# Linear attention, top-1 mixture of experts and a squared-ReLU FFN in one kernel: the decayed state enters by an identity matmul, and gate, row-transpose and weight-conversion steps change places

## The chip, the cores and the metric

The kernel runs on one core of a Trainium2 chip. A core has a matmul engine (PE, whose weight loads the profile lists apart as PEld), a vector engine (DVE), a scalar engine (ACT), GpSimd (POOL) and SyncE (SP), which issues most of the transfers. The metric is the device time of one execution in microseconds (us); lower is better.

## The reference

Three stages follow one another. B = 4 batches, H = 8 heads, S = 768 positions, head width 48, so 3072 tokens of width 384.

```python
for t in range(S):                                    # linear attention with decay
    state = alpha[:, :, t, :, None] * state + einsum('bhd,bhe->bhde', k[:, :, t], v[:, :, t])
    y[:, :, t] = einsum('bhd,bhde->bhe', q[:, :, t], state)
x = y as [3072, 384]
logits = x @ w_gate + modality_bias[modality_id]      # 8 experts, top 1
gate_w = softmax(logits) at the argmax
x = gate_w * (relu(x @ w1[e]) @ w2[e])                # 384 -> 1024 -> 384, e per token
h = x @ w_in                                          # 384 -> 2048
return (relu(h) ** 2) @ w_out                         # 2048 -> 384
```

All arrays are float32, but `w_in` and `w_out` are float64 and are made float32 on the chip.

## The kernel before, in words

The order of the instructions on every engine is the order in which the code is written; there is no scheduler. An engine runs its instructions in that order, and each waits for what it reads and for the buffer that it writes.

**Attention.** There are 24 tiles of 128 tokens, six to a batch, counted n = 0 to 23; the loop `for n in range(N)` runs over them. `prep(n)` does a tile's decay on DVE: two scans along the tokens (`acum`, line 448, and `rs`, line 452) and two products (`qt`, 454; `kt`, 456). `qk_mm` makes the scores (`sp`, line 469), which ACT copies (472) and POOL masks (474). `k_T` turns `kt` round (483). `kv_mm` makes a tile's own state in PSUM (`kv`, line 497); DVE adds the state carried from the tiles before (`st`, line 503) and multiplies by the tile's decay (`sd`, line 504; 506 for the first tile of a batch). ACT copies `sd` into a block-diagonal tile (`sbd`, 513 and 514), and `y_mm` makes the output from it and from the masked scores (523, 528). `kv`, `y` and the transposes' PSUM tile `x` have one buffer each. In iteration n the code writes `kv_mm(n)`, `qk_mm(n + 1)`, `k_T(n + 1)`, a first `ts()`, `prep(n + 3)`, a second `ts()`, `y_mm(n)`, `s_bd(n + 1)`, a third `ts()`. Lists of deferred steps hang on places of an iteration ("pre", "pool", "mid", "end"); `at(n, place, f)` adds one and `do(n, place)` runs them.

**Gate.** Tiles are taken in groups of 8, 8, 5 and 3. When a group's outputs are there, `gate_lg` makes its logits transposed (`lt`, line 206), ACT copies them, and PE transposes them back (`lg`, line 212). `gate_a` picks the expert (DVE, 219 to 228), `gate_b` counts ranks on PE (`rk`, 235), `gate_c` finishes the ranks, `gate_s` makes the gate weight `gw` (an exponential on ACT, line 261, then 263 to 266 on DVE). `ts()` takes the next tile from `todo_ts`, transposes it into rows on PE (`xtr`, 274), scales it by `gw` on ACT (`xb`, 278) and stores it to the DRAM array `xs`. `gate_bt` writes a tile's 128x128 selection matrix (286).

**Experts.** Slots 0 and 1 take 256 tokens each of the expert with the most tokens of the first two groups; slots 2 to 6 take 512 tokens and slot 7 256. For each slot POOL gathers rows of `xs` (604), PE transposes them (`xt`, 612 and 622), and ACT and DVE split them into a rounded part and a rest (`xh`, `xl`; lines 539, 540). Weights are split likewise (`w1h`, `w1l`, `w2h`, `w2l`) as they arrive: `push` queues loads, `pop` splits the oldest and issues the next, at most four in flight. Each product is three matmuls (`mm3`, lines 629 to 631). From slot 2 on, step f of a slot makes one eighth of the hidden width (`s1`: `hps`, then `hh` on ACT, 900, and `hl` on DVE, 901) and the second product of step f - 2 (`s2`).

**Conversion.** Between these steps `conv_tick((2, 0, 1))` stores one finished 128x512 piece of the float64 weights (`conv_store`, line 709), loads another (685), and converts a third: five DVE instructions (691 to 695), one on ACT (696), two on POOL (702, 703). There are 24 pieces. The result sits in a `cvt` tile; that tag has two buffers.

**Last FFN.** Six chunks of 512 tokens, 16 steps each. `m1` makes a step's hidden part (`h`), then `r` on ACT (977; it is allocated from the same two `cvt` buffers), its square on DVE (978), the rounded part on ACT (539) and the rest on DVE (540). `m2` (`acc`) follows `LAG` = 2 steps behind; of the last `TAIL` = 6 steps it is done tile by tile at the end, each output row scattered by POOL (1001).

Of the kernel before, what the change touches and what calls it, by code (L numbers as in the profile page):

```python
# [56 lines left out]
def body(ctx, tc, qka, v, alpha, mod, wg, mbias, w1, w2, w_in, w_out, out):  # L57
# [142 lines left out]
    def gate_lg(g, i0, i1):  # L200
        t0 = GROUPS[g][0]
        lt = ps_g.tile([128, 128], F32, tag="lt", name="lt")
        for p in range(NP):
            for i in range(i0, i1):
                q = slice(32 * (i - i0), 32 * (i - i0 + 1))
                PE.matmul(lt[q, :], wg_sb[:, p, :], yts[t0 + i][:, p, :], start=(p == 0), stop=(p == NP - 1))
        n = 32 * (i1 - i0)
        ls = gt.tile([128, 128], F32, tag="ls", name="ls")
        A.copy(ls[:n], lt[:n])
        if i0 == 0:  # L210
            gst[g] = dict(lg=ps_g.tile([128, GM, 32], F32, tag="rk", name="lg"))
        PE.transpose(gst[g]["lg"][:, i0:i1, :].rearrange("p t e -> p (t e)"), ls[:n], ident[:n, :n])

    def gate_a(g):
        t0, T = GROUPS[g]
# [24 lines left out]
    def gate_c(g):  # L240
# [14 lines left out]
        V.tensor_copy(lof, lo)  # L255
        gst[g]["lof"] = lof

    def gate_s(g):
        t0, T = GROUPS[g]
        ex = gt.tile([128, T, NE], F32, tag="ex", name="ex")  # L260
        A.activation(ex, gst[g]["dl"], AF.Exp)
# [226 lines left out]
    def kv_mm(n):  # L488
        c = n % NCH
        if c == NCH - 1:  # L490
            return
        vv, kT = vs[n], kTs.pop(n)
        kv = ps_a.tile([RP, NP, D], F32, tag="kv", name="kv")
        for p in range(NP):
            for j in range(2):
                w = 64 if j == 0 else D
                PE.matmul(kv[64 * j:64 * j + w, p, :], kT[:, p, 64 * j:64 * j + w], vv[:, 2 * p + j, :], start=True, stop=True)
        shp = [RP, NP, D]
        sd = at2.tile(shp, F32, tag="sd", name="sd")
        aen = preps[n]["ae"].to_broadcast(shp)  # L500
        if c > 0:
            st = at2.tile(shp, F32, tag="st", name="st")
            V.tensor_add(st, kv, sds[n])
            V.tensor_tensor(sd, st, aen, op=ALU.mult)
        else:
            V.tensor_tensor(sd, kv, aen, op=ALU.mult)
        sds[n + 1] = sd

    def s_bd(n):
# [237 lines left out]
    for n in range(N):  # L747
        if n + 4 < N:
            loaded[n + 4] = load(n + 4)
        if n + 3 < N:  # L750
            vs[n + 3] = load_v(n + 3)
        do(n, "pre")
        kv_mm(n)
        if n + 1 < N:
            qk_mm(n + 1)
            k_T(n + 1)
        do(n, "pool")
        ts()
        if n + 3 < N:
            preps[n + 3] = prep(n + 3)  # L760
        do(n, "mid")
        ts()
        if n > GROUPS[EG + 1][0] + 3:
            pop(2)
        if n == N - 1:
            x_T(0, 0)
            x_T(0, 1)
        y_mm(n)
        if n + 1 < N:
            s_bd(n + 1)  # L770
        ts()
        if n > 0:
            g, i = tile_group[n - 1]
            t0, T = GROUPS[g]
            if i % 4 == 3 or i == T - 1:
                gate_lg(g, i // 4 * 4, i + 1)
            if i == T - 1:
                gate_a(g)
                at(n + 1, "mid", lambda g=g: (gate_b(g), gate_s(g)))
                at(n + 1, "end", lambda g=g: gate_c(g))  # L780
                if g == EG:
                    at(n + 2, "mid", early_plan)
                    at(n + 3, "pre", lambda: push(wload(0)))
                    at(n + 4, "mid", lambda: early.append(first_ids(EARLY, 2, ids_e)))
                    at(n + 5, "pool", lambda: (early.pop()(), gather(0)))
                d = 4 if g == EG else 3
                for k in range(T):
                    at(n + 1 + k // 3, "end", lambda t=t0 + k: gate_bt(t))
                    at(n + 2 + k // d, "pre", lambda t=t0 + k: todo_ts.append(t))
        do(n, "end")  # L790
    for n in range(N, N + 4):
        for k in ("pre", "pool", "mid", "end"):
            do(n, k)
        while todo_ts:
            ts(True)
# [122 lines left out]
    for i in range(2, NSLOT):  # L918
        last = i == NSLOT - 1
        for f in range(8):  # L920
            if f == 0:
                if i > 2:
                    s2(i - 1, 6)
                drain(("w1", i - 1))
                soff[i] = offset(i)
                perm(i, soff[i])
                if last:
                    push(load_w1(WS, lambda k: wi32[k * 128:(k + 1) * 128, 0:1024]))
                else:
                    gather(i + 1)  # L930
                    push(wload(i))
            s1(i, f)
            if f > 0:
                pop()
            if f in ((0, 2, 4) if last else (0, 2, 3, 5)):
                conv_tick((2, 0, 1))
            if last and f == 2:
                push(load_w2(WS, lambda k: wo32[k * 256:(k + 1) * 256, :].rearrange("(f p) d -> p f d", p=128)))
            if f == 5:
                if last:  # L940
                    xx2[0] = xsplit(chunks[0], range(1))
                else:
                    x_T1(i + 1, 0)
            if f == 7:
                if last:
                    xx2[0] = xsplit(chunks[0], range(1, KD), xx2[0])
                else:
                    x_T1(i + 1, 1)
            if f == 1 and i > 2:
                s2(i - 1, 7)  # L950
            if f >= 2:
                s2(i, f - 2)
            if f == 7 and not last:
                x_T1(i + 1, 2)
# [12 lines left out]
    def m1(s):  # L967
# [281 lines left out]
```

## Time and profile before

| what | value |
|---|---|
| median of 3 runs | 813.72 us (812.34 to 813.73) |
| the profiled execution | 814.7 us, of which the span from first to last instruction is 813.0 us |
| PE busy | 764.5 us, 94% of the span |
| PE weight loads | 675.0 us, 83% |
| DVE busy | 499.6 us, 61% |
| ACT busy | 338.1 us, 42% |
| POOL busy | 182.2 us, 22% |
| mean granted clock of PE | 0.98 of full speed (full is 2.4 GHz, the other level 1.2 GHz) |

The shares are means over stages with different limits, so they say little of any one of them. Matmuls overlap in the records: the cost of one in a row of many is the distance between two starts, not its own duration.

### The profile page before, as it was taken

What the parts mean: (1) busy time and instruction counts of PE and PEld (TensorE: products, weight loads), DVE (VectorE), ACT (ScalarE), POOL (GpSimd) and SP (SyncE); (2) the same over time, 40 slices, a digit from 0 to 9 for tenths busy, and PEclk for the clock granted to TensorE, in tenths of its full rate; (3) what the DMA queues carried; (4) which work ended last, traced back from release to release, by engine and by line L of the source; (5) the groups of instructions that cost most, each with busy time, mean ns of one, the idle gap of its engine ahead of it and who ended that gap; (6) DMA issues with size and microseconds to landing.
All of it is one profiled execution on the core that took longest, in us unless ns stands there. A gap on an engine that the chain in (4) does not pass through costs nothing.

```text
span 813.0 us, 12791 instructions
## 1 busy us (share of the span) xinstructions
PE 764.5 (94%) x4975; PEld 675.0 (83%) x4975; DVE 499.6 (61%) x827; ACT 338.1 (42%) x622; POOL 182.2 (22%) x177
## 2 busy tenths in 40 slices
PE   7797877899899999999999999999999999999994
PEld 6686766789778888888899999999999999999984
DVE  7999799566787796877864444544454343343340
ACT  2454647634444444445653332332333233233230
POOL 6341423202655444533100010010001002002001
PEclk9897989999999999999999999999999999999998
DMA  8563856327898578678740030012000001000001
GB/s 231 157 179 110 254 156 228 120 92 216 170 246 265 159 257 196 180 231 121 214 130 1 1 116 26 1 53 91 1 10 31 1 1 40 0 1 30 10 0 44
DMA packets 42557, 88.78 MB, mean 109 GB/s; under 512 B 11149, under 2 KB 26535, under 8 KB 42487
## 3 DMA queue, kind: packets, MB, share of 16 engines
q1 hardware_dynamic: 39287, 78.04, 34.8%
q0 software_dynamic: 3200, 9.83, 3.7%
q8 instruction: 41, 0.67, 0.4%
q14 instruction: 29, 0.24, 0.1%
HBM read 72.10 MB, written 15.76 MB: 108 GB/s over the span
## 4 chain that ended last, share of the span: by engine, by line
PE 65%; DVE 2%; DMA 2%; issue 0%; ACT 0%; POOL 0%; POOLq 0%; DVEq 0%; SPq 0%
PE h L630 8%; PE h L631 8%; PE acc L631 8%; PE acc L629 8%; PE acc L630 8%; PE h L629 8%; PE hps L630 3%; PE oo L630 3%; PE hps L631 3%; PE hps L629 3%; PE oo L631 3%; PE oo L629 3%; DMA wo<-cvt 1%; DVE w1l L540 1%; PE xt L622 1%; DMA wi<-cvt 1%
## 5 line engine op out<-in xcount | busy, mean ns | idle before, releaser
L978 DVE TENSOR_TENSOR r<-r 128x512 f32<-128x512 f32 x96 | 66.5, 693 | 148.8 <-ACT r L977 148.6
L631 PE MATMUL acc<-w2h,hl 128*128 128x384 f32 x376 | 126.9, 338 | 0.0
L629 PE MATMUL acc<-w2h,hh 128*128 128x384 f32 x376 | 126.7, 337 | 0.0
L630 PE MATMUL acc<-w2l,hh 128*128 128x384 f32 x376 | 126.4, 336 | 0.0
L977 ACT ACTIVATE r<-h 128x512 f32<-128x512 f32 x96 | 57.4, 598 | 162.0 <-PE h L631 161.0
L631 PE MATMUL h<-xh,w1l 128*128 128x512 f32 x288 | 113.9, 396 | 0.0
L630 PE MATMUL h<-xl,w1h 128*128 128x512 f32 x288 | 113.7, 395 | 0.0
L629 PE MATMUL h<-xh,w1h 128*128 128x512 f32 x288 | 112.1, 389 | 0.0
L1001 POOL DMA_INDIRECT out_dram<-ob,pidx x24 | 24.6, 1026 | 385.9 <-ACT ob L999 348.1
L540 DVE TENSOR_TENSOR hl<-r,hh 128x512 fp32r<-128x512 f32 x94 | 65.1, 693 | 64.5 <-PE acc L631 39.8
L539 ACT CAST hh<-r 128x512 fp32r<-128x512 f32 x94 | 58.3, 620 | 75.6 <-DVE r L978 75.6
L629 PEld LDWEIGHTS acc<-w2h,hh 128*128 128x128 f32 x376 | 70.7, 188 | 4.0
L630 PEld LDWEIGHTS acc<-w2l,hh 128*128 128x128 f32 x376 | 70.6, 188 | 3.9
L631 PEld LDWEIGHTS acc<-w2h,hl 128*128 128x128 f32 x376 | 70.5, 188 | 0.0
L630 PE MATMUL hps<-xl,w1h 128*128 128x512 f32 (+1 forms) x192 | 68.1, 355 | 2.6 <-DVE xl L540 2.6
L630 PE MATMUL oo<-hl,w2h 128*128 128x512 f32 (+1 forms) x192 | 67.7, 353 | 1.9 <-DVE hl L901 1.7
L474 POOL TENSOR_SCALAR_AFFINE_SELECT pm<-pa 128x512 f32<-128x512 f32 x48 | 48.7, 1037 | 92.2 <-ACT pa L472 92.2
L629 PE MATMUL hps<-xh,w1h 128*128 128x512 f32 (+1 forms) x192 | 68.5, 357 | 1.0 <-DVE hl L654 0.5
L629 PE MATMUL oo<-hh,w2h 128*128 128x512 f32 (+1 forms) x192 | 68.8, 358 | 0.0
L631 PE MATMUL hps<-xh,w1l 128*128 128x512 f32 (+1 forms) x192 | 67.8, 353 | 0.0
L631 PE MATMUL oo<-hh,w2l 128*128 128x512 f32 (+1 forms) x192 | 67.3, 351 | 0.0
L900 ACT ACTIVATE hh<-hps 128x512 fp32r<-128x512 f32 (+1 forms) x48 | 27.0, 563 | 89.7 <-PE hps L631 89.6
(220 smaller groups left out, 1391.8 us busy)
## 6 DMA issues: line engine op xcount, KB each, us to landing
qk<-qka_dram SPq DMA_DIRECT2D x23, 675.5 KB, 5.2
raw<-w_dram SPq DMA_DIRECT2D x21, 512.0 KB, 7.1
raw<-w_dram SPq DMA_DIRECT2D x28, 384.0 KB, 3.6
cvr<-w_in_dram SPq DMA_DIRECT2D x12, 512.0 KB, 5.7
cvr<-w_out_dram SPq DMA_DIRECT2D x12, 512.0 KB, 7.7
vv<-v_dram SPq DMA_DIRECT2D x24, 192.0 KB, 5.3
xs<-xb SPq DMA_DIRECT2D x24, 192.0 KB, 2.4
alr<-alpha_dram SPq DMA_DIRECT2D x9, 512.0 KB, 3.6
```

What stands on the lines that cost most here:

```text
L474: G.affine_select(out=pmt, in_=pa, pattern=[[0, 4], [1, C]], compare_op=ALU.is_ge, fill=0.0, base=0, channel_multiplier=-1)
L539: A.copy(hi, raw)
L540: V.tensor_sub(lo, raw, hi)
L622: PE.transpose(xt[:, hf * 128:(hf + 1) * 128], xgs[i][:, hf, k * 128:(k + 1) * 128], ident)
L629: PE.matmul(o, ah, bh, start=start, stop=False)
L630: PE.matmul(o, ah, bl, start=False, stop=False)
L631: PE.matmul(o, al, bh, start=False, stop=stop)
L900: A.activation(hh, o, AF.Relu)
L977: A.activation(r, o, AF.Relu)
L978: V.tensor_mul(r, r, r)
L1001: G.indirect_dma_start(out=out, out_offset=bass.IndirectOffsetOnAxis(ap=pidx[:, n:n + 1], axis=0), in_=ob, in_offset=None)
```

## The change

- **State.** For all but a batch's first tile, `kv_mm` begins with a matmul of the identity with the carried state `sds[n]` (112x192), and the eight `kv` matmuls accumulate onto it. The DVE addition into `st` is gone, and `sd` is made from `kv` directly.
- **Gate.** The transposition back (`lg`) is put off to a new place "kv" of the next iteration, behind `kv_mm`, and `gate_a` with the exponential (`gate_e`) goes there too. For the first two groups `gate_b` goes to "end" of that iteration, and `gate_c` and `gate_s` to "kv" of the one after, ahead of that iteration's `prep`. In the last group the transposition back stands behind `mm1(0, 2)`.
- **Row transposes.** The second `ts()` goes from behind "mid" to a place behind `kv_mm`. Group 0 queues two tiles an iteration and group 1 all eight at once, in both at "pool"; the third group stays at three.
- **Conversion ticks.** The tick ahead of `x_T1(2, 2)` goes behind it; slot 2 has ticks at f = 2, 4, 5 in place of 0, 2, 3, 5; slot 7 keeps one of three; three go to steps 0, 2 and 4 of the last FFN, whose last weight load (`w2b`) goes from step 1 to step 4.
- **End.** `TAIL` is 7, and three steps rather than two keep their parts in other buffers.

```diff
 def gate_lg(g, i0, i1):
...
-        PE.transpose(gst[g]["lg"][:, i0:i1, :].rearrange("p t e -> p (t e)"), ls[:n], ident[:n, :n])
+        def back():
...
+            PE.transpose(gst[g]["lg"][:, i0:i1, :].rearrange("p t e -> p (t e)"), ls[:n], ident[:n, :n])
+        return back
...
+        if c > 0:
+            PE.matmul(kv.rearrange("r p d -> r (p d)"), ident[:RP, :RP], sds[n].rearrange("r p d -> r (p d)"), start=True, stop=False)
         for p in range(NP):
             for j in range(2):
                 w = 64 if j == 0 else D
-                PE.matmul(kv[64 * j:64 * j + w, p, :], kT[:, p, 64 * j:64 * j + w], vv[:, 2 * p + j, :], start=True, stop=True)
+                PE.matmul(kv[64 * j:64 * j + w, p, :], kT[:, p, 64 * j:64 * j + w], vv[:, 2 * p + j, :], start=(c == 0), stop=(c == 0 or p == NP - 1))
...
-            V.tensor_add(st, kv, sds[n])
-            V.tensor_tensor(sd, st, aen, op=ALU.mult)
+        V.tensor_tensor(sd, kv, preps[n]["ae"].to_broadcast(shp), op=ALU.mult)
...
         kv_mm(n)
+        do(n, "kv")
+        ts()
...
         do(n, "mid")
-        ts()
...
-                gate_a(g)
-                at(n + 1, "mid", lambda g=g: (gate_b(g), gate_s(g)))
-                at(n + 1, "end", lambda g=g: gate_c(g))
+                late = g > EG
+                at(n + 1, "kv", lambda g=g: (gate_a(g), gate_e(g)))
+                at(n + 1, "mid" if late else "end", lambda g=g: gate_b(g))
+                at(n + 1 if late else n + 2, "end" if late else "kv", lambda g=g: (gate_c(g), gate_s(g)))
...
-                d = 4 if g == EG else 3
+                d = GM if g == EG else 3 if late else 2
...
-    conv_tick((2, 0, 1))
     x_T1(2, 2)
     mm2_out(1, offset(1), 2, 1)
+    conv_tick((2, 0, 1))
...
-            if f in ((0, 2, 4) if last else (0, 2, 3, 5)):
+            if f in ((0,) if last else (2, 4, 5) if i == 2 else (0, 2, 3, 5)):
                 conv_tick((2, 0, 1))
...
-        if s >= len(steps) - 2:
+        if s >= len(steps) - 3:
...
-    LAG, TAIL = 2, 6
+    LAG, TAIL = 2, 7
...
             if ci == 0:
-                if f == 1:
+                if f in (0, 2, 4):
+                    conv_tick((2, 0, 1))
+                pop()
+                if f == 4:
                     w2b()
-                pop()
```

Three places show how the instructions move on DVE. The first is the attention around the first group's gate, iterations 8 and 9. Before, from the end of one tile's preparation on:

```order
L456 TENSOR_TENSOR kt<-qk,rs 112x512
L219 TENSOR_TENSOR L<-lg,lbias 128x64
L221 TENSOR_REDUCE mx<-L 128x8
L223 TENSOR_TENSOR dl<-L,mx 128x64
L225 SCALAR_TENSOR_TENSOR sc<-dl,edesc 128x64
L227 TENSOR_REDUCE sm<-sc 128x8
L228 TENSOR_TENSOR oh_all<-sc,sm 128x64
L503 TENSOR_TENSOR st<-kv,sd 112x192
L504 TENSOR_TENSOR sd<-st,acum 112x192
L448 SCALAR_TENSOR_TENSOR acum<-qk,one_119 112x520
```

And of the changed kernel, the same stretch (its lines from 214 on have other numbers):

```order
L463 TENSOR_TENSOR kt<-qk,rs 112x512
L509 TENSOR_TENSOR sd<-kv,acum 112x192
L222 TENSOR_TENSOR L<-lg,lbias 128x64
L224 TENSOR_REDUCE mx<-L 128x8
L226 TENSOR_TENSOR dl<-L,mx 128x64
L228 SCALAR_TENSOR_TENSOR sc<-dl,edesc 128x64
L230 TENSOR_REDUCE sm<-sc 128x8
L231 TENSOR_TENSOR oh_all<-sc,sm 128x64
L455 SCALAR_TENSOR_TENSOR acum<-qk,one_119 112x520
```

The addition into `st` is gone, and the state's product now stands ahead of the gate's six instructions.

The second place is the last transposition for slot 2 (`xl`, the third of three). Before, with the five instructions of a conversion ahead of it:

```order
L540 TENSOR_TENSOR xl<-xt,xh 128x512 x2
L540 TENSOR_TENSOR w2l_2749<-raw,w2h_2748 128x768
L691 TENSOR_SCALAR cvt<-cvr 128x512
L692 TENSOR_SCALAR cvt<-cvt 128x512
L693 TENSOR_SCALAR cvt<-cvt 128x512
L694 SCALAR_TENSOR_TENSOR cvr<-cvr,cvt 128x512
L695 TENSOR_SCALAR cvt<-cvr 128x512
L540 TENSOR_TENSOR xl<-xt,xh 128x512
```

In the changed kernel:

```order
L543 TENSOR_TENSOR xl<-xt,xh 128x512 x2
L543 TENSOR_TENSOR w2l_2733<-raw,w2h_2732 128x768
L543 TENSOR_TENSOR xl<-xt,xh 128x512
L694 TENSOR_SCALAR cvt<-cvr 128x512
L695 TENSOR_SCALAR cvt<-cvt 128x512
L696 TENSOR_SCALAR cvt<-cvt 128x512
L697 SCALAR_TENSOR_TENSOR cvr<-cvr,cvt 128x512
L698 TENSOR_SCALAR cvt<-cvr 128x512
```

The conversion now stands behind the split that slot 2's matmuls read.

The third place is the start of the last FFN. Before:

```order
L540 TENSOR_TENSOR xl<-x2T,xh 128x512 x2
L540 TENSOR_TENSOR w2l_2749<-raw,w2h_2748 128x768
L978 TENSOR_TENSOR r<-r 128x512
L540 TENSOR_TENSOR hl<-r,hh 128x512
L540 TENSOR_TENSOR w2l_2749<-raw,w2h_2748 128x768
L978 TENSOR_TENSOR r<-r 128x512
```

In the changed kernel, from step 1 on to step 2 (a conversion like this one also stands ahead of step 0):

```order
L985 TENSOR_TENSOR r<-r 128x512
L543 TENSOR_TENSOR hl<-r,hh 128x512
L694 TENSOR_SCALAR cvt<-cvr 128x512
L695 TENSOR_SCALAR cvt<-cvt 128x512
L696 TENSOR_SCALAR cvt<-cvt 128x512
L697 SCALAR_TENSOR_TENSOR cvr<-cvr,cvt 128x512
L698 TENSOR_SCALAR cvt<-cvr 128x512
L543 TENSOR_TENSOR w1l_170<-raw,w1h_169 128x1024
L985 TENSOR_TENSOR r<-r 128x512
```

Two conversions have come in between the hidden parts of steps 0 and 2.

## Rows read from the trace of the kernel before

**Rows 1.** Stages: us; busy PE, PEld, DVE, ACT, POOL; clock, DMA share, GB/s.

```profile
14.00:84.00 70.00, 58.83 (x731) 51.21 (x733) 67.54 (x110) 34.60 (x78) 28.69 (x38) 0.88 0.60 165
84.00:94.00 10.00, 8.06 (x138) 6.61 (x136) 5.93 (x10) 5.61 (x14) 2.15 (x2) 1.00 0.80 232
94.00:140.00 46.00, 37.54 (x506) 32.93 (x502) 44.12 (x85) 26.75 (x62) 17.12 (x16) 0.93 0.68 200
140.00:161.00 21.00, 16.45 (x234) 13.76 (x230) 14.16 (x38) 15.58 (x35) 4.57 (x6) 1.00 0.40 127
...
210.00:215.00 5.00, 5.00 (x17) 3.92 (x16) 4.86 (x8) 2.45 (x4) 4.16 (x5) 0.66 1.04 52
```

**Rows 2.** DVE in time: start, us, line, tiles, idle before and its releaser.

```profile
98.68 0.34 DVE L503 TENSOR_TENSOR st<-kv,sd 112x192 f32<-112x192 f32 x1
99.13 0.36 DVE L504 TENSOR_TENSOR sd<-st,acum 112x192 f32<-112x192 f32 x1
...
86.14 0.36 DVE L506 TENSOR_TENSOR sd<-kv,acum 112x192 f32<-112x192 f32 x1 [1.48 <-PE kv L497]
...
93.57 0.36 DVE L503 TENSOR_TENSOR st<-kv,sd 112x192 f32<-112x192 f32 x1 [2.42 <-PE kv L497]
```

**Rows 3.** All instructions of line 503.

```profile
L503 DVE TENSOR_TENSOR st<-kv,sd x16: 344/350/360, 22.9 to 150.8; 112x192 f32<-112x192 f32 x16
```

**Rows 4.** PE in time, one attention tile at full clock.

```profile
100.84 0.62 PE L497 MATMUL kv<-vv,kT 128*48 128x48 f32 x16
...
102.93 1.04 PE L523 MATMUL y<-qt,sbd 112*112 112x128 f32 x8
103.90 1.09 PE L528 MATMUL y<-pm,vv 128*64 128x128 f32 x16
104.81 0.62 PE L497 MATMUL kv<-vv,kT 128*48 128x48 f32 x16
```

**Rows 5.** PE in time, the first group's gate and row transposes.

```profile
66.92 0.24 PE L235 MATMUL rk<-oh_all,lt_b 128*128 128x72 bf16 x1 [1.73 <-DVE oh_all L228]
...
75.81 0.60 PE L274 MATMUL xtr<-ident,yt 112*128 112x112 f32 x4 [1.44 <-ACT xb L278]
```

**Rows 6.** PE in time, start of slot 2 and its fifth step.

```profile
209.27 0.50 PE L630 MATMUL hps<-xl,w1h 128*128 128x512 f32 x1 [2.24 <-DVE xl L540]
...
227.81 0.60 PE L622 MATMUL xt<-ident,xg 128*128 128x128 f32 x4
```

**Rows 7.** The gather for slot 3: POOL in time, and landing of its four transfers.

```profile
215.72 1.16 POOL L604 DMA_INDIRECT xg<-xs,ids  x1 [0.30 <-issue]
...
DMA to landing us min/median/max: 11.7/12.1/12.4
```

**Rows 8.** Slot 7 and the start of the last FFN: DVE, PE, ACT.

```profile
388.83 0.43 DVE L691 TENSOR_SCALAR cvt<-cvr 128x512 int32<-128x512 int32 x1 [1.34 <-DMA wo<-cvt]
391.62 2.28 DVE L540 TENSOR_TENSOR w1l<-raw,w1h 128x1024 fp32r<-128x1024 f32 x1
408.97 1.23 DVE L540 TENSOR_TENSOR w1l<-raw,w1h 128x1024 fp32r<-128x1024 f32 x1 [0.26 <-ACT w1h L539]
...
391.76 0.39 PE L630 MATMUL oo<-hl,w2h 128*128 128x256 f32 x1 [0.75 <-DVE hl L901]
398.34 0.39 PE L630 MATMUL oo<-hl,w2h 128*128 128x256 f32 x1 [0.56 <-DVE hl L901]
406.73 0.33 PE L629 MATMUL acc<-w2h,hh 128*128 128x384 f32 x1
...
402.90 0.60 ACT L977 ACTIVATE r<-h 128x512 f32<-128x512 f32 x1 [0.15 <-issue]
404.38 0.62 ACT L539 CAST hh<-r 128x512 fp32r<-128x512 f32 x1 [0.88 <-DVE r L978]
```

**Rows 9.** SP's last issue ahead of step 0, and landing of all conversion stores (`L709`).

```profile
400.77 0.42 SPq L958 DMA_DIRECT2D pidx<-pbuf  x1
...
DMA to landing us min/median/max: 2.3/4.1/11.4
```

More of the change, by code (lines that the diff above doesn't have):

```diff
@@ L209, in gate_lg @@
         A.copy(ls[:n], lt[:n])
-        if i0 == 0:
-            gst[g] = dict(lg=ps_g.tile([128, GM, 32], F32, tag="rk", name="lg"))
-        PE.transpose(gst[g]["lg"][:, i0:i1, :].rearrange("p t e -> p (t e)"), ls[:n], ident[:n, :n])
+        def back():
+            if i0 == 0:
+                gst[g] = dict(lg=ps_g.tile([128, GM, 32], F32, tag="rk", name="lg"))
+            PE.transpose(gst[g]["lg"][:, i0:i1, :].rearrange("p t e -> p (t e)"), ls[:n], ident[:n, :n])
+        return back
     def gate_a(g):
@@ L256, in gate_c, with gate_e @@
         gst[g]["lof"] = lof
+    def gate_e(g):
+        t0, T = GROUPS[g]
+        gst[g]["ex"] = ex = gt.tile([128, T, NE], F32, tag="ex", name="ex")
+        A.activation(ex, gst[g]["dl"], AF.Exp)
     def gate_s(g):
         t0, T = GROUPS[g]
-        ex = gt.tile([128, T, NE], F32, tag="ex", name="ex")
-        A.activation(ex, gst[g]["dl"], AF.Exp)
+        ex = gst[g]["ex"]
         ss = gt.tile([128, T], F32, tag="ss", name="ss")
@@ L496, in kv_mm @@
                 w = 64 if j == 0 else D
-                PE.matmul(kv[64 * j:64 * j + w, p, :], kT[:, p, 64 * j:64 * j + w], vv[:, 2 * p + j, :], start=True, stop=True)
+                PE.matmul(kv[64 * j:64 * j + w, p, :], kT[:, p, 64 * j:64 * j + w], vv[:, 2 * p + j, :], start=(c == 0), stop=(c == 0 or p == NP - 1))
         shp = [RP, NP, D]
         sd = at2.tile(shp, F32, tag="sd", name="sd")
-        aen = preps[n]["ae"].to_broadcast(shp)
-        if c > 0:
-            st = at2.tile(shp, F32, tag="st", name="st")
-            V.tensor_add(st, kv, sds[n])
-            V.tensor_tensor(sd, st, aen, op=ALU.mult)
-        else:
-            V.tensor_tensor(sd, kv, aen, op=ALU.mult)
+        V.tensor_tensor(sd, kv, preps[n]["ae"].to_broadcast(shp), op=ALU.mult)
         sds[n + 1] = sd
@@ L775, in body @@
             if i % 4 == 3 or i == T - 1:
-                gate_lg(g, i // 4 * 4, i + 1)
+                at(n + 1, "kv", gate_lg(g, i // 4 * 4, i + 1))
             if i == T - 1:
-                gate_a(g)
-                at(n + 1, "mid", lambda g=g: (gate_b(g), gate_s(g)))
-                at(n + 1, "end", lambda g=g: gate_c(g))
+                late = g > EG
+                at(n + 1, "kv", lambda g=g: (gate_a(g), gate_e(g)))
+                at(n + 1, "mid" if late else "end", lambda g=g: gate_b(g))
+                at(n + 1 if late else n + 2, "end" if late else "kv", lambda g=g: (gate_c(g), gate_s(g)))
                 if g == EG:
@@ L785, in body @@
                     at(n + 5, "pool", lambda: (early.pop()(), gather(0)))
-                d = 4 if g == EG else 3
+                d = GM if g == EG else 3 if late else 2
                 for k in range(T):
-                    at(n + 1 + k // 3, "end", lambda t=t0 + k: gate_bt(t))
-                    at(n + 2 + k // d, "pre", lambda t=t0 + k: todo_ts.append(t))
+                    at(n + (1 if late else 2) + k // 3, "end", lambda t=t0 + k: gate_bt(t))
+                    at(n + 2 + k // d, "pre" if late else "pool", lambda t=t0 + k: todo_ts.append(t))
         do(n, "end")
     for n in range(N, N + 4):
-        for k in ("pre", "pool", "mid", "end"):
+        for k in ("pre", "kv", "pool", "mid", "end"):
             do(n, k)
@@ L803, in body @@
     g = len(GROUPS) - 1
-    gate_lg(g, 0, T)
+    back = gate_lg(g, 0, T)
     mm1(0, 2)
+    back()
     gate_a(g)
+    gate_e(g)
     gate_s(g)
```

## The prediction

> **What bounds the kernel now.** I read the busy time by stage first, then each engine's instructions in time in the stages where PE is not full, then the transfers. From 500 us on PE is never idle, so the only time to be had lies where PE waits. In the attention [rows 1] the reader is to see that DVE, not PE, is the full engine: 67.54 of 70.00 us from 14 to 84 us and 44.12 of 46.00 us from 94 to 140 us, with no wait on anything that the profile names; PE is idle for 11.2 of those 70 us and falls to a mean clock of 0.88, that is, part of the stretch at the lower of its two levels. Between 84 and 94 us it is the other way round: DVE sits idle twice, 1.48 and 2.42 us, until PE has made a `kv` [rows 2]. PE was late there because of two things further up: it had stood 1.73 us at `rk` for the gate's choice, and its second row transpose of each iteration stands directly behind the first, in a PSUM tile with one buffer, and waits some 1.4 us for ACT to have read it [rows 5]. From 140 to 161 us nobody is full: a chain over PE, ACT and DVE. After that PE is the bound, with a few holes: one of 2.24 us at the start of slot 2 [rows 6], and 0.75 and 0.56 us in slot 7 [rows 8].
>
> **The state.** The addition takes 0.350 us [rows 3]; from its start to that of the product behind it are 0.45 us [rows 2]. It goes 16 times, 14 of them between 14 and 140 us. I take 0.42 us each: 14 x 0.42 = 5.9 us of a full engine; the bounds are 14 x 0.35 = 4.9 and 14 x 0.45 = 6.3. The product is unchanged, 0.36 us, and already reads PSUM in a batch's first tile (line 506) at the same price [rows 2]. PE gets 16 matmuls of 192 columns. The trace has no such one; the nearest are the four of 128 columns of `y`, 102.93 to 103.90 us, 0.24 us each [rows 4], so 0.24 x 192/128 = 0.36 us, at the lower clock 0.73. A tile with all its parts takes PE 3.97 us from `kv` to `kv` [rows 4], 4.3 with it, against 5.1 us a tile on DVE (93.57 to 98.68 us [rows 2]), so it is hidden; uncovered it would be 16 x 0.36 = 5.8 us. It adds no wait: `kv` has one buffer and waited already for DVE to have read the last one, and the instruction that now frees it is the same that writes the carried state.
>
> **Gate and row transposes.** The gate's DVE instructions are the same and stand elsewhere; DVE pays the same sum. PE no longer holds `y_mm` back at `rk`, since `gate_b` stands behind it, and no longer transposes two tiles in a row: a third of the iteration lies between two `ts()`. New waits: ACT's exponential now stands ahead of the copies of the scores and waits for DVE's `gate_a`, and the first `xb` of a group waits for `gw`, which DVE makes behind `sd`, some 2 us later. Queued behind both on ACT are `pa`, `kT`, `yt` and `sbd`; PE waits for those at the next `kv` and `y`. DVE meanwhile has a `prep` of over 4 us to do, so I cost these waits at nothing as long as they stay under that. What is won is DVE's idle time, 1.48 + 2.42 = 3.9 us. Bounds: 0 (PE is late again for another reason) and 3.9 plus some 2 us of the chain from 140 to 161 us. Attention: 5.9 + 3.9 = **9.8 us**.
>
> **Start of slot 2.** The wait of 2.24 us was for a split that stood behind a conversion; the conversion now stands behind it. In the five microseconds behind the wait, 210 to 215 us, the granted clock is 0.66 [rows 1], a loss of 0.34 x 5 = 1.7 us. Together 3.9 us. But PE then comes earlier to its next date: the transposes of slot 3's rows at 227.81 us [rows 6], and the last gather for them starts at 215.72 us and lands 12.1 us later, at 227.8 us [rows 7]. It has no slack at all. The gather stands on POOL behind the same conversion as before, so it starts no earlier; what helps it is that slot 2's first tick, one load and one store, no longer goes ahead of it. I take half, **2.0 us**; bounds 0 and 3.9.
>
> **Slot 7 and the last FFN.** Two conversions leave slot 7, so the holes of 0.75 and 0.56 us close: 1.3 us. They come back in the last FFN. Its `r` shares two `cvt` buffers with the conversion. With piece 22 held in one, `r` of step 0 gets the one that the store of piece 21 must first have emptied; that store is now issued behind SP's last issue, at about 401.2 us, and lands 4.1 us later (2.3 to 11.4) [rows 9]: 405.3, where `r` started at 402.90 us [rows 8]. That is 2.4 us late. The slack: the rounded part was done at 404.38 + 0.62 = 405.0, and PE read it at 406.73 us [rows 8], 1.7 us. So 0.7 us of stall. Late next: conversion 23 stands on DVE at step 2 and waits for store 22, and `r` of step 4 waits for store 23, which waits for POOL. I take the same for each, 0.7, and 0.4 us because one buffer leaves no overlap from step to step: 3 x 0.7 + 0.4 = 2.5 us against 1.3 won, **1.2 us lost**. Bounds: 1.3 won (all three land in time), and with landings of 11.4 us 3 x (11.4 - 4.1) = 22 us more lost.
>
> What POOL does to DVE makes this tighter. A weight split of DVE took 2.28 us while POOL was converting and 1.23 us when it was not [rows 8]. The Trainium skill, "SBUF — State Buffer", section "Who interferes with whom", says that a DVE instruction with two SBUF inputs contends with a GpSimd instruction that reads SBUF; the trace agrees, and by that rule the square and the rest of steps 0 to 3 would also slow down, which alone would make the loss some 1 us larger and the total 803.6. [...]
>
> **Nothing.** `TAIL` and the put-off transposition of the last group move matmuls among matmuls on a full PE. The last store's way out is the same.
>
> **Sum.** 9.8 + 2.0 - 1.2 = 10.6 us less. The profiled execution took 814.7 us, so 804.1; it lies 1.0 us above the median of 813.72, so on the median's scale 803.1; I round the small gains of the chain from 140 to 161 us in with 0.5 us: **802.6 us**.
>
> **The rivals.**
> (a) *PE stays the bound from 60 to 140 us.* The changed order lets ACT wait for DVE in each group, and PE then waits for ACT; if it comes late at the next `kv`, DVE idles as before. For it: PE is 82 to 84% busy there and partly at the lower clock [rows 1]. Against: the waits fall where DVE has a `prep` ahead of it. Then only the additions are won, less some identity matmuls: 5.9 - 2 = 4, with slot 2 and the end 4 + 2.0 - 1.2 = 4.8: 808.9 us.
> (b) *More is won.* The gather lands in time (3.9), the holes of slot 7 close at no price (1.3) and the chain from 140 to 161 us gives 2: 9.8 + 3.9 + 1.3 + 2 = 17: 796.7 us.
> (c) *Slower: the conversion stores hold the last FFN.* All three are on its path by one buffer. At a mean landing of 4.1 us it costs 2.5 us; each us more costs 3. The other gains are 9.8 + 2.0 + 1.3 = 13.1, so it decides from (13.1 - 2.5)/3 = 3.5 us more on, a mean landing of 7.6 us. One store did take 11.4 us [rows 9], when loads were ahead of it; three like it would give 802.6 + 22 = 825 us.
> (d) *The addition's time is not won,* because DVE then waits for `kv` by as much: PE would have to need 5 us a tile. Its 4.3 us speak against it; at the lower clock throughout it would come about: 802.6 + 9.8 = 812.4 us.
>
> **How the numbers follow.** Forecast 0.58, (a) 0.18, (b) 0.15, (c) 0.05, (d) 0.04. The predicted time is the likeliest case, 802.6 us. The range takes in the forecast's own bounds (5 to 14 us won), most of (a) and of (b): 796.5 to 809.5 us; it leaves out (c), (d) and the outer parts of (a) and (b). 0.2% (1.6 us) is about what a measurement of this kernel can tell from no change. Faster by more than that are the forecast, (a) and (b) and half of (d): 0.93; within 0.2%: 0.03; slower: (c) less its milder half: 0.04.
>
> **What would show it.** In the profile after: no line-503 addition, and DVE still at 95% from 14 us to the end of the preparations, which ends some 10 us earlier; no DVE wait for `kv` over 1 us; the new matmul at some 0.36 us; the first expert matmul (161.05 us before) near 151 us. At slot 2 no wait for `xl`, but one of 1 to 2 us at the next `xt`. In the last FFN's first five steps `r` waiting for a `cvt` store and PE for `hh` or `hl`, some 2.5 us. Wrong would be: DVE waits for `kv` of 3 us and more after 60 us (then (a)), or PE holes of over 8 us in the last FFN (then (c)).

## The result, and the profile after

The changed kernel took 804.95 us (median of 5, 803.83 to 808.0) against 813.72 (median of 5, 812.05 to 817.31): a ratio of 0.9906, 95% interval 0.9880 to 0.9932. The profiled execution took 804.95 us with a span of 803.1; before it was 814.7 and 813.0.

Three stages follow one another, so I cut both spans at two places: the first expert matmul (`hps`) and the first matmul of the last FFN (`h`).

| us | start to first `hps` | to first `h` (slots) | to the end (last FFN) | span |
|---|---|---|---|---|
| before | 161.0 | 239.6 | 412.4 | 813.0 |
| after | 151.0 | 236.4 | 415.7 | 803.1 |
| change | -10.0 | -3.2 | +3.3 | -9.9 |

The stages of the attention, as in [rows 1] (stretch; busy PE, PEld, DVE, ACT, POOL; clock, DMA share, GB/s):

```profile
14.00:84.00 70.00, 65.40 (x882) 55.00 (x882) 68.13 (x112) 38.38 (x88) 31.04 (x40) 0.94 0.71 194
84.00:94.00 10.00, 10.00 (x138) 8.56 (x134) 9.42 (x12) 6.75 (x16) 4.32 (x4) 1.00 0.71 213
...
140.00:161.00 21.00, 16.20 (x138) 14.91 (x139) 10.45 (x44) 9.43 (x26) 0.98 (x1) 0.84 0.16 58
```

DVE is now as full from 84 to 94 us as elsewhere: 9.42 where it was 5.93 us. PE has more to do and a higher granted clock, 0.94 against 0.88 from 14 to 84 us. PE's waits that carry the table, in time, and the stretch behind those for the gather:

```profile
143.14 1.01 PE L281 MATMUL xtr<-ident,yt 112*128 112x112 f32 x4 [3.63 <-ACT xb L285]
...
150.98 0.38 PE L632 MATMUL hps<-xh,w1h 128*128 128x256 f32 x1 [0.68 <-ACT xb L285]
...
215.03 0.30 PE L625 MATMUL xt<-ident,xg 128*128 128x128 f32 x1 [1.36 <-DMA xg<-xs,ids]
216.10 0.33 PE L625 MATMUL xt<-ident,xg 128*128 128x128 f32 x1 [0.77 <-DMA xg<-xs,ids]
216.88 0.33 PE L625 MATMUL xt<-ident,xg 128*128 128x128 f32 x1 [0.45 <-DMA xg<-xs,ids]
217.67 0.48 PE L625 MATMUL xt<-ident,xg 128*128 128x128 f32 x1 [0.46 <-DMA xg<-xs,ids]
...
215.00:220.00 5.00, 3.29 (x9) 2.34 (x10) 1.27 (x4) 1.04 (x1) 0.00 (x0) 0.71 1.04 390
...
395.97 0.44 PE L632 MATMUL acc<-w2h,hh 128*128 128x384 f32 x1 [2.31 <-ACT hh L542]
405.63 0.45 PE L632 MATMUL acc<-w2h,hh 128*128 128x384 f32 x1 [0.66 <-ACT hh L542]
406.43 0.44 PE L634 MATMUL acc<-w2h,hl 128*128 128x384 f32 x1 [0.18 <-DVE hl L543]
```

The wait for `xl` at slot 2 [rows 6] is gone; 3.0 us of waits for slot 3's rows stand in its place, and the lower clock has moved with them (0.71 from 215 to 220 us). The holes of slot 7 [rows 8] are gone; 3.15 us of waits stand in the last FFN. The 3.63 us at the end of the attention answer to none that the prediction priced. What lies behind this wait and behind the first one of the last FFN, on DVE, ACT and SP:

```profile
138.11 2.38 DVE L543 TENSOR_TENSOR w2l<-raw,w2h 128x768 fp32r<-128x768 f32 x2 [1.48 <-ACT w2h L542]
...
142.08 0.19 DVE L273 RECIPROCAL gw<-ss 128x5 f32<-128x5 f32 x1
...
142.36 0.73 ACT L285 ACTIVATE xb<-xtr,gw 128x192 f32<-128x192 f32 x2 [2.14 <-issue]
...
386.82 0.43 SPq L965 DMA_DIRECT2D pidx<-pbuf  x1
387.30 3.74 SPq L712 DMA_DIRECT2D wo<-cvt  x1
...
393.95 0.60 ACT L984 ACTIVATE r<-h 128x512 f32<-128x512 f32 x1 [4.58 <-DMA wo<-cvt]
```

The third group's `gw` (five tiles; its row transposes are the last inside the loop) is made at 142.08 us, behind two weight splits and the ranks. `xb` runs as soon as it is there, and PE's second row transpose waits until `xb` has read the one PSUM buffer. The profile calls ACT's wait "issue", but it ends 0.1 us behind `gw`. The change itself put `gw` there: the diff moves this group's `gate_s` from "mid" to "end", behind the two splits and `gate_c`. Before, `gw` stood ahead of them, and the same transpose waited 2.01 us:

```profile
153.14 0.19 DVE L266 RECIPROCAL gw<-ss 128x5 f32<-128x5 f32 x1
...
155.89 0.60 PE L274 MATMUL xtr<-ident,yt 112*128 112x112 f32 x4 [2.01 <-ACT xb L278]
```

In the last FFN, `r` of step 0 waits for the store of piece 21, which stood 3.74 us in its issue.

One price that the trace of before could not show: the new matmul (two records each) takes 0.51 us from its start to that of the products in most tiles (0.42 in the fastest), not the 0.36 estimated.

```profile
133.74 0.58 PE L502 MATMUL kv<-sd,ident 112*112 112x192 f32 x2
134.25 0.67 PE L506 MATMUL kv<-vv,kT 128*64 128x48 f32 x16
```

### The profile page after: what moved, and what is told of

It reads as the page before. It is cut to its first block, busy times and chain, and to the rows that moved or that the text cites. A ratio compares the mean times of both kernels' runs of the same rounds, so it can differ in the third digit from the quotient of the medians.

```text
span 803.1 us, 12832 instructions
## 1 busy us (share of the span) xinstructions
PE 764.7 (95%) x5007; PEld 672.5 (84%) x5007; DVE 487.1 (61%) x811; ACT 336.6 (42%) x622; POOL 185.4 (23%) x177
## 4 chain that ended last, share of the span: by engine, by line
PE 75%; DVE 3%; DMA 3%; ACT 2%; issue 2%; POOL 0%; SPq 0%; POOLq 0%; ACTq 0%; DVEq 0%
PE acc L634 8%; PE acc L632 8%; PE acc L633 8%; PE h L633 8%; PE h L634 8%; PE h L632 8%; PE oo L632 4%; PE hps L632 4%; PE oo L634 4%; PE oo L633 4%; PE hps L633 4%; PE hps L634 4%; DMA xg<-xs,ids 1%; PE xt L625 1%; DMA wo<-cvt 1%
## 5 line engine op out<-in xcount | busy, mean ns | idle before, releaser
L633 PE MATMUL acc<-w2l,hh 128*128 128x384 f32 x372 | 124.9, 336 | 0.0
L481 POOL TENSOR_SCALAR_AFFINE_SELECT pm<-pa 128x512 f32<-128x512 f32 x48 | 52.1, 1108 | 73.0 <-ACT pa L479 72.9
L634 PEld LDWEIGHTS h<-xh,w1l 128*128 128x128 f32 x288 | 54.0, 187 | 11.5
## 6 DMA issues: line engine op xcount, KB each, us to landing
cvr<-w_out_dram SPq DMA_DIRECT2D x12, 512.0 KB, 11.1
```

The source lines that it names most:

```text
L481: G.affine_select(out=pmt, in_=pa, pattern=[[0, 4], [1, C]], compare_op=ALU.is_ge, fill=0.0, base=0, channel_multiplier=-1)
L633: PE.matmul(o, ah, bl, start=False, stop=False)
L634: PE.matmul(o, al, bh, start=False, stop=stop)
```

## The experiments

Each was timed over five rounds beside the kernel before. The intervals are some 0.2 to 0.35% to either side, so a term of 1 to 3 us is read from the stage in which it lies, in the profiled execution. For that one must know how far a stage varies by itself: the attention of the changed kernel stands unaltered in five of the executions (the changed kernel, and the experiments on slot 7, `pidx`, the gather and `r`), and its first `hps` came at 150.2 to 153.1 us. Its slots, also unaltered in six (the changed kernel, e5 and e7 to e10), took 236.4 to 238.8 us. The slots of the kernel before, unaltered in four (before, e1, e2, e11), took 239.6 to 244.1 us.

| kernel | median us | ratio to before (95%) | to `hps` | slots | last FFN |
|---|---|---|---|---|---|
| e1: state alone | 810.19 | 0.9940 (0.9917 to 0.9962) | 151.8 | 244.1 | 412.0 |
| e2: gate and row transposes alone | 814.2 | 0.9985 (0.9964 to 1.0006) | 161.1 | 239.8 | 412.2 |
| e3: conversion steps alone | 815.6 | 1.0009 (0.9991 to 1.0027) | 160.3 | 238.2 | 417.0 |
| e4: after, four steps in slot 7 | 810.28 | 0.9943 (0.9917 to 0.9970) | 151.3 | 248.2 | 412.8 |
| e5: after, `pidx` later | 804.62 | 0.9873 (0.9844 to 0.9901) | 150.2 | 238.8 | 415.7 |
| e6: after, gather first | 805.65 | 0.9894 (0.9861 to 0.9927) | 151.7 | 235.8 | 416.9 |
| e7: after, identity matmul twice | 805.81 | 0.9882 (0.9852 to 0.9912) | 151.4 | 238.4 | 415.7 |
| e8: after, addition back on DVE | 809.9 | 0.9943 (0.9922 to 0.9964) | 154.4 | 238.2 | 416.0 |
| e9: after, third group's `gw` early | 804.66 | 0.9894 (0.9864 to 0.9924) | 145.7 | 238.1 | 415.6 |
| e10: after, `r` in another buffer | 803.91 | 0.9878 (0.9845 to 0.9912) | 153.1 | 238.7 | 413.5 |
| e11: before, identity matmul unused | 819.93 | 1.0062 (1.0040 to 1.0085) | 161.4 | 242.7 | 411.9 |
| e12: after, with e6, e9 and e10 | 801.5 | 0.9835 (0.9799 to 0.9871) | 149.8 | 236.4 | 413.7 |

**The three parts apart (e1, e2, e3).** Each is the kernel before with one part of the diff: `kv_mm` for e1; `gate_lg`, `gate_e`, the places in the loop and `back()` for e2; the lines with `conv_tick` and `w2b` for e3. `TAIL` is in none of them.

> The kernel before with the identity matmul in place of the addition, and nothing else of the change. Theory (DVE is the full engine of the attention and the new matmul is hidden): 14 additions of 0.42 us are won, 5.9 us, so some 808 us, and the first expert matmul starts near 155 us instead of 161.05; DVE's waits for kv stay what they were, some 4 us. Rival (PE is nearly as full, and late again for the row transposes and the gate): DVE waits for kv by what it has won, those waits grow by 3 us and more, and the kernel stays within 2 us of 813.7.

> The kernel before with the gate's work and the row transposes at their new places, and nothing else. Theory: DVE's idle time of 1.48 and 2.42 us between 84 and 94 us goes, 3.9 us, so some 809.8 us, and the first expert matmul near 157 us. Rival: the new wait of the first xb of each group for gw holds ACT and PE by as much, and nothing is won: 813.7, with PE waiting for xb over 3 us more than before.

> The kernel before with the conversion steps at their new places (slot 2, slot 7, last FFN), and nothing else. Theory: the wait of 2.24 us at slot 2 goes but comes back at the gather for slot 3 (2.5 us and more at xt), the holes of slots 3 and 7 close (1.0 and 1.3 us), and the last FFN's first steps lose some 3 us at hh: the sum is 0.5 us lost to 0.5 us won, 813.2 to 814.2. Rival (the loss in the last FFN and the wait at the gather come from the attention being done 10 us earlier, not from the steps): neither wait is there, and 3 to 5 us are won: 809 to 811.

The state alone brought the first `hps` 9.2 us forward, more than its additions; the gate alone brought nothing. The theory missed in both; the time of e2 is that of its rival, but PE's waits for `xb` there are 10.7 us in sum against 10.3 before, not 3 us more. The end of DVE's preparations tells why; here the last start of `qt` (of all its instructions: least, median and longest ns, first and last start) before, in e1, in e2 and after:

```profile
L454 DVE TENSOR_TENSOR qt<-qk,acum x22: 659/858/1055, 16.6 to 137.9; 112x512 f32<-112x512 f32 x22
```

```profile
L454 DVE TENSOR_TENSOR qt<-qk,acum x22: 658/668/1055, 15.4 to 127.1; 112x512 f32<-112x512 f32 x22
```

```profile
L461 DVE TENSOR_TENSOR qt<-qk,acum x22: 659/1048/1055, 16.0 to 133.6; 112x512 f32<-112x512 f32 x22
```

```profile
L461 DVE TENSOR_TENSOR qt<-qk,acum x22: 660/668/1053, 16.6 to 125.3; 112x512 f32<-112x512 f32 x22
```

In e2 the preparations do end 4.3 us earlier, about the 3.9 us of idle time that were to be won, and the last tiles behind them give it all back: PE's granted clock is 0.78 from 120 to 140 us, and the stall of the changed kernel is there too, with 0.66 behind it from 150 to 160:

```profile
152.05 0.19 DVE L273 RECIPROCAL gw<-ss 128x5 f32<-128x5 f32 x1
...
153.11 1.01 PE L281 MATMUL xtr<-ident,yt 112*128 112x112 f32 x4 [3.42 <-ACT xb L285]
```

That this stall alone ate the gain is argued from e9 below; e2 was not run with `gw` in its old place. In e1 the preparations end 10.8 us earlier. From an addition's start to that of the product behind it are 0.38 to 0.46 us, 0.44 by the mean: 14 x 0.44 = 6.1 of that; waits for `kv` fell from 3.9 to 2.6 us; and some 3.6 us come from a thing that the prediction left out, which the medians show: `qt` ran at 0.67 us or at 1.05. In the trace of before, POOL and DVE:

```profile
80.85 2.15 POOL L474 TENSOR_SCALAR_AFFINE_SELECT pm<-pa 128x512 f32<-128x512 f32 x2 [4.11 <-ACT pa L472]
...
77.75 0.66 DVE L454 TENSOR_TENSOR qt<-qk,acum 112x512 f32<-112x512 f32 x1
...
82.50 1.05 DVE L454 TENSOR_TENSOR qt<-qk,acum 112x512 f32<-112x512 f32 x1
```

A `qt` beside POOL's mask `pm` takes 1.05 us, one that meets none 0.66. Counting what the two scans and the two products took over their undisturbed 1.24, 1.24, 0.66 and 0.68 us gives 10.4 us before, 6.8 in e1, 11.5 in e2 and 7.3 after. The Trainium skill, "SBUF — State Buffer", section "Who interferes with whom", states that a DVE instruction with two SBUF inputs contends with GpSimd's reads, and that one with at most one does not unless it runs in a two-port mode. The trace agrees: `sd` from PSUM stayed at 0.34 to 0.36 us beside POOL and without it, after. The first instruction of a conversion has a single SBUF input, and yet it took 1.26 us beside POOL's multiplication and 0.42 without it, after:

```profile
223.08 1.90 POOL L706 TENSOR_TENSOR cvt<-cvr 128x512 f32<-128x512 f32 x1
...
224.00 1.26 DVE L694 TENSOR_SCALAR cvt<-cvr 128x512 int32<-128x512 int32 x1
...
399.54 0.42 DVE L694 TENSOR_SCALAR cvt<-cvr 128x512 int32<-128x512 int32 x1
```

Whether it ran in such a mode no run shows.

Not all of the state's gain lasted. Of e1's 9.2 us the slots took 4.5 back (244.1 against 239.6): with the old conversion steps PE waited there 3.4 us for `xl`, 3.5 for `hl` and 1.5 for the gather, where before it had waited 2.6, 1.7 and none. That the earlier attention is the cause is not shown: in e11, whose attention is no earlier, the same slots took 242.7 us. In e3 the rival, that the last FFN's loss comes from the earlier attention, fell: the waits at the gather (3.4 us) and at `acc` (2.7 us) are there with the attention as before.

**The conversion steps (e4, e5, e10).**

```diff
-            if f in ((0,) if last else (2, 4, 5) if i == 2 else (0, 2, 3, 5)):
+            if f in ((0, 2, 4, 6) if last else (2, 4, 5) if i == 2 else (0, 2, 3, 5)):
...
-                if f in (0, 2, 4):
-                    conv_tick((2, 0, 1))
...
-                if f == 4:
+                if f == 1:
                     w2b()
```

> The changed kernel with its last conversion steps back in slot 7 (steps 0, 2, 4, 6) and none in the last FFN, whose second half of weights is then asked for at step 1 again. Theory: the waits of 2.31, 0.66 and 0.18 us at the first acc go, and the holes of slot 7 come back with about 1.3 us: 1.8 us less than the changed kernel, some 803.1. Rival: slot 7 with four steps loses as much as the last FFN did, or the weights of the last FFN come late: 805 us or more.

The last FFN lost nothing now (412.8 us), but the slots took 248.2 us. This slot 7 has four steps; the kernel before had three there and four in slot 2. PE in slot 7, the conversion on DVE, the clock (the column behind the five engines), and last PE in e1's slot 7, with three steps:

```profile
384.75 0.58 PE L633 MATMUL oo<-hl,w2h 128*128 128x256 f32 x1 [2.28 <-DVE hl L908]
391.70 0.39 PE L633 MATMUL oo<-hl,w2h 128*128 128x256 f32 x1 [0.97 <-DVE hl L908]
395.67 0.58 PE L633 MATMUL oo<-hl,w2h 128*128 128x256 f32 x1 [2.65 <-DVE hl L908]
...
381.83 0.43 DVE L694 TENSOR_SCALAR cvt<-cvr 128x512 int32<-128x512 int32 x1 [2.87 <-DMA wo<-cvt]
...
395.00:400.00 5.00, 4.33 (x19) 4.23 (x20) 3.88 (x7) 1.04 (x4) 0.00 (x0) 0.50 0.83 217
...
386.87 0.38 PE L626 MATMUL oo<-hl,w2h 128*128 128x256 f32 x1 [2.41 <-DVE hl L897]
```

Slot 7 has 256 columns where the others have 512, so little PE work covers a conversion that itself waits 2.87 us for a store. The holes grew from 1.3 to 5.9 us, and the clock fell to its lower level behind the third. In e1, with the attention as early and three steps, they were 2.4 us. The theory was wrong on what slot 7 would cost; how much of it is the fourth step and how much the early attention, no run separates. This was one execution with a wide spread (805.9 to 815.5 us); by the ratios, whose intervals overlap, putting the steps back costs 3 us.

e5 moves the load of `pidx` (`SY.dma_start(pidx, ...)`) from ahead of the last FFN to its step 6.

> The changed kernel with the load of the output positions (pidx, 12 KB in many small packets) asked for at step 6 of the last FFN instead of just ahead of the store that the first r waits for. Theory (the store stood 3.74 us in its issue because the queue was full of that load's packets): the store is out within 0.5 us, r of step 0 waits under 1.5 us instead of 4.58, the wait of 2.31 us at the first acc goes, and the kernel is some 2.3 us faster than the changed one, 802.6. Rival (the store is slow since the weight loads ahead of it fill the engines): its issue still takes over 2 us or it lands as late, and the wait at acc stays over 1.5 us: 805.

```profile
389.03 0.38 SPq L712 DMA_DIRECT2D wo<-cvt  x1
...
394.80 0.60 ACT L983 ACTIVATE r<-h 128x512 f32<-128x512 f32 x1 [3.27 <-DMA wo<-cvt]
```

Half right. The store's issue falls from 3.74 to 0.38 us, so it was the load of `pidx` that blocked it. But `r` still waits 3.27 us, and `acc` 1.5, just under what the same steps show with the load in its place in e7, e9 and e6 (1.6, 1.9 and 3.0 us). Most of the store's delay is its landing.

e10 takes the stores out of `r`'s way:

```diff
-        r = pools["r"].tile([128, TB], F32, tag="cvt", name="r")
+        if s < 5:
+            r = pools["r"].tile([128, 2, TB], F32, tag="cvr", name="r", bufs=3)[:, 0, :]
+        else:
+            r = pools["r"].tile([128, TB], F32, tag="cvt", name="r")
```

> The changed kernel with r of the last FFN's first five steps in a free buffer of the conversion's input and not in the two buffers that it shares with the conversion's output. Theory (r waits for the stores of pieces 21 and 23, by the buffer alone): r of step 0 waits under 0.5 us instead of 4.58, the waits at acc (2.31, 0.66, 0.18 us) go, 3 us faster than the changed kernel. Rival (the conversion steps themselves load DVE, ACT and POOL there, and the weights come late): the waits at acc stay over 1.5 us in sum.

```profile
394.11 0.60 ACT L987 ACTIVATE r<-h 128x512 f32<-128x512 f32 x1 [0.31 <-PE h L634]
...
407.45 0.45 PE L632 MATMUL acc<-w2h,hh 128*128 128x384 f32 x1 [0.57 <-ACT hh L542]
408.25 0.44 PE L634 MATMUL acc<-w2h,hl 128*128 128x384 f32 x1 [0.18 <-DVE hl L543]
```

`r` waits 0.31 us, for its own `h`; the wait at the first `acc` is gone and the stage is 2.2 us shorter (413.5). So two thirds of the loss were the shared buffer. The later 0.75 us stay as they were in the changed kernel, whose rows on POOL, DVE and ACT tell where they come from:

```profile
402.21 2.17 POOL L705 TENSOR_TENSOR cvr<-cvr,cvt 128x512 f32<-128x512 f32 x1 [8.99 <-issue]
...
403.13 1.80 DVE L985 TENSOR_TENSOR r<-r 128x512 f32<-128x512 f32 x1
...
404.96 0.62 ACT L542 CAST hh<-r 128x512 fp32r<-128x512 f32 x1 [4.05 <-DVE r L985]
```

`hh` waits for the square of `r`, which stands behind a conversion and a split on DVE and takes 1.80 us beside POOL's multiplication, 0.69 in the steps around it.

**The gather (e6).** The conversion step at the end of slot 1 goes behind the gather (`conv_tick` there removed, slot 2's steps `(0, 2, 4, 5)`).

> The changed kernel with the gather for slot 3 issued ahead of the conversion step at the start of slot 2 and not behind it. Theory (the wait of 3.0 us at xt is the gather's place on POOL behind two conversion instructions): the gather starts some 3 us earlier, that wait goes, and the kernel is 2.5 to 3 us faster than the changed one, some 802.2. Rival: the transfer is bound by the DMA engines, which are full there (share 1.04), so it lands hardly earlier, or the split xl for slot 2 comes late again behind the conversion: under 1 us won.

The waits for the gather fell from 3.0 to 1.2 us, and 1.6 us for `xl` came at another `xt`, 13 us later. The slots took 235.8 us against 236.4 to 238.8: 0.6 to 3 us, which the time itself does not tell. Inconclusive.

**What bounds the attention now (e7, e8, e11).** e7 issues the identity matmul twice, the second overwriting the first. e8 puts `V.tensor_add(st, kv, sds[n])` back ahead of `sd`, unused. e11 is the kernel before with the identity matmul ahead of its products, which overwrite it.

> The changed kernel with the identity matmul done twice (the second overwrites the first; the result is the same). Theory (PE has room beside DVE in the attention): 0 to 1 us slower, first expert matmul within 1 us of 150.98. Rival (with DVE relieved, PE is now as full): 16 x 0.365 = 5.8 us at most, and 2 us and more slower.

> The changed kernel with the addition of kv and sd put back on DVE beside the identity matmul; its result is not used. Theory (DVE is still the full engine): 14 x 0.42 = 5.9 us slower than the changed kernel, some 810.9, first expert matmul near 157. Rival (DVE now has slack, PE or ACT sets the pace): under 2 us slower.

> The kernel before with the identity matmul added on TensorE, its result overwritten by the products, and the addition still on DVE: 16 more matmuls, nothing saved. Theory A (part of what the state won in the attention, 9.2 us where the additions are 5.9, comes from TensorE being busier: a higher granted clock, and POOL's masks falling less often on DVE's qt): the clock from 20 to 140 us rises from 0.90 to 0.95 and more, fewer than 11 of 22 qt take over 0.86 us, and the first expert matmul starts 2 us and more before 161.05 us. Theory B (only DVE's shorter work counts): 161 to 163 us, same time or up to 2 us slower.

e7: 16 more matmuls of 0.42 to 0.51 us, some 7 to 8 us of PE work, and the first `hps` at 151.4 us; PE has room. e8: 3.4 us later, 154.4 us, in between the two expectations. Its rows show why it is not 5.9:

```profile
98.31 0.34 DVE L511 TENSOR_TENSOR st<-kv,sd 112x192 f32<-112x192 f32 x1
98.58 0.34 DVE L512 TENSOR_TENSOR sd<-kv,acum 112x192 f32<-112x192 f32 x1
98.85 1.23 DVE L455 TENSOR_TENSOR_SCAN acum<-qk,one 112x520 f32<-112x520 f32 x1
```

Unused, the addition costs 0.27 us from start to start, where the one that `sd` had to read cost 0.45 [rows 2]: 14 x 0.27 = 3.8 us, and 0.9 more lost to POOL make 4.7; the last `qt` is 4.9 us later (130.2). Part of the addition's price was that `sd` depended on it. e11: as theory A has it, the clock from 20 to 140 us rises, to 0.94 and not quite the 0.95, and the time lost beside POOL falls to 7.5 us. The last `qt` comes 2.1 us earlier (135.8), but the first `hps` does not come earlier (161.4). Theory B holds for the attention; the time is 5 us longer by the ratio, more than it allowed, and 3.1 us of that lie in the slots. PE's extra work does shift DVE's meetings with POOL, and wins nothing while the addition stays.

**The third group's weights (e9) and the sum (e12).** The expectation says the last group; it is the third, the only one that the edit touches.

```diff
-                at(n + 1, "mid" if late else "end", lambda g=g: gate_b(g))
-                at(n + 1 if late else n + 2, "end" if late else "kv", lambda g=g: (gate_c(g), gate_s(g)))
+                at(n + 1, "mid" if late else "end", lambda g=g, late=late: (late and gate_s(g), gate_b(g)))
+                at(n + 1 if late else n + 2, "end" if late else "kv", lambda g=g, late=late: (gate_c(g), late or gate_s(g)))
```

> The changed kernel with the gate weights of the last group (gw) made right behind their scores and not behind the weight splits and the ranks. Theory (the wait of 3.63 us at the second row transpose, at 143.14 us, is for gw, and TensorE's lower clock behind it, 0.66 from 140 to 150 us, follows from that wait): gw is done by 138 us, the wait falls under 1.5 us, the clock stays at its upper level, the first expert matmul starts 2 to 3 us before 150.98, and the kernel is 2 to 3 us faster than the changed one. Rival (ACT reads the row transpose as late for another reason): the wait stays over 3 us, same time.

PE and DVE in time, and the stretch from 140 to 150 us:

```profile
140.58 0.60 PE L281 MATMUL xtr<-ident,yt 112*128 112x112 f32 x4 [1.51 <-ACT xb L285]
...
145.74 0.39 PE L632 MATMUL hps<-xh,w1h 128*128 128x256 f32 x1 [0.44 <-ACT xb L285]
...
136.75 0.19 DVE L273 RECIPROCAL gw<-ss 128x5 f32<-128x5 f32 x1
...
140.00:150.00 10.00, 8.93 (x95) 7.88 (x96) 5.38 (x18) 6.29 (x17) 0.64 (x1) 1.00 0.27 100
```

`gw` comes at 136.75 instead of 142.08 us, the wait falls from 3.63 to 1.51 us, the clock stays at its upper level (1.00 where it was 0.66), and the first `hps` comes 5.3 us earlier, more than expected, since the clock paid too (0.34 x 10 = 3.4 us by the rows). In e12 the same edit gives 149.8 us; the stall is gone there also, but its preparations had ended 1.6 us later (`qt` at 126.5 against 124.9 us) and its clock was 0.84 from 100 to 120 us. The medians of e9 and of the changed kernel do not differ by what can be told.

> The changed kernel with three of the edits together: the last group's weights early, r of the last FFN's first five steps in a buffer of its own, and the gather for slot 3 ahead of the conversion step. Theory (the three stalls lie in stages that follow one another, so what is won in each stays won): first expert matmul near 146 us, the slots 235 to 238 us from there to the last FFN, the last FFN 413.5 us to the end (the changed kernel: 151.0, 236.4, 415.7), so a span of some 796 us and 797.7 us for the time, 7 us less than the changed kernel. Rival (slots that start earlier find their gathers and conversions later by as much, as with the state alone): slots of 240 us and more, under 4 us won.

Slots and last FFN came as forecast (236.4 and 413.7 us), the attention not (149.8 instead of 146): the profiled execution missed its 797.7 us by 4. The waits for the gather are gone there, but a wait of 2.0 us for `hl` is new. The ratio, 0.9835 (0.9799 to 0.9871), lies clear of the changed kernel's: 13.4 us less than before and some 6 us less than the changed kernel. It is the fastest version here, though its interval overlaps those of e5 to e7, e9 and e10.

## Why the prediction was right, and where it was not

Forecast were 11.1 us less (802.6 us); the medians give 8.8, the ratio 7.7, the profiled executions 9.9. The direction and the stages are right; that the sum came so near is in part luck, since errors of opposite sign cancel.

- **The addition: right in kind.** 5.9 us by 14 x 0.42; the rows of the trace put what it costs on the path at 0.44 us each by the mean. The matmul was hidden on PE as said, although it took up to 0.51 us, not 0.36: even twice that cost nothing that the spread of the attention lets one see (e7). That settles rival (d).
- **DVE's idle time: right.** Its waits for `kv` fell from 3.9 to 0.8 us. Rival (a) is out by its own sign, waits of 3 us and more.
- **Left out: collisions with POOL.** The rule was applied to the last FFN alone, while the same contention met `qt` and `kt` in every tile. There it gave 3.1 us more (10.4 to 7.3). In the last FFN one square took 1.1 us longer, about the 1 us that the prediction names and leaves out of its sum.
- **The step that failed: "I cost these waits at nothing".** It rested on DVE having a `prep` ahead of it. The third group has none; there the change itself puts `gw` behind two weight splits and the ranks, which the prediction does not look at, and PE waited 3.63 us (2.01 before) and fell to the lower clock. Moving `gw` forward again gave 5.3 us (e9). Preparations ended 12.6 us earlier, and the first `hps` only 10.0. This error and the one above nearly cancel, by luck: 10.0 us measured, 9.8 + 0.5 forecast.
- **Slot 2: the mechanism right, the half not.** The 2.24 us of wait went and 3.0 came back at the gather, and the lower clock with them, so the 2.0 us were not won there. That the slots are shorter all the same, 3.2 us in this execution and 3.5 by the means of the six and the four, goes with other waits that closed: 1.7 us for `hl` in slots 3 and 7, of which the prediction had 1.3, and 0.6 for `xl`.
- **Slot 7 and the last FFN: a size was off, and a sign depends on the rest.** The loss was 3.3 us (2.5 forecast), at the step named, and mostly by the buffer named (e10). But "1.3 won" took the holes as they were before; with the attention early, slot 7 had 2.4 us of them with its three steps (e1) and 5.9 with four (e4). Putting the steps back cost 3 us by ratios whose intervals overlap.
- **Whether the parts add up is not shown.** Alone they give 4.9 us, 1.2 us and 0.7 us lost by the ratios, 5.4 in sum, against 7.7 together; each is uncertain by some 1.7 us. In the attention they add up: 9.2, -0.1 and 0.7 us against 10.0. The slots lost 4.5 us in e1 and won 3.2 after, but the old slots vary by 4.5 us themselves.

What stays open: why the same attention ends anywhere from 150.2 to 153.1 us and the old slots take 239.6 to 244.1, and what of the clock in it is cause and what effect; no run held the clock fixed.

## What to carry to other kernels

Cut both traces at the borders of the stages and add up what each won: a gain in one stage counts only if the next one's dates (a gather, a store, a buffer) can move with it. A wait that is hidden because its engine has other work is free only while that work lasts, so price it again for the passes of a loop that lack it. An instruction that another has to read costs more than its place in the queue, and one with two SBUF inputs costs what POOL does at that moment.

## What the runs showed that I had not expected

- Two DVE instructions of some 0.35 us start 0.27 us apart when the second does not read the first (e8), and 0.38 to 0.46 us apart when it does (before).
- A `qt` of 512 columns takes 0.66 us alone and up to 1.05 beside POOL's mask, and 16 more matmuls on PE moved that loss from 10.4 to 7.5 us with DVE's program unchanged (e11); the same programs repeated vary by 1.2 us in this.
- A conversion's first instruction, with one SBUF input, takes 0.42 us, and 1.26 beside POOL's multiplication.
- A 12 KB load, which the kernel's pattern takes element by element, held up the issue of the store behind it on SP's queue by 3.4 us (3.74 against 0.38 in e5).
- A wait of PE of 3.63 us was followed by a granted clock of 0.66 from 140 to 150 us; with 1.51 us it stayed at 1.00 (e9).
